# A visit's squares behind the next h copy on VectorE, h blocks strictly one after another, and a later first visit for batch 2

## The chip, the cores and the metric

The kernel runs on one core of a Trainium2 chip. The metric is the device time of one execution in microseconds (us); the time before is the median of eleven runs. Everything said of single instructions comes from one profiled execution.

## The reference

Eight batches of a squared-ReLU attention (12 heads, 448 positions, head size 64) feed one feed-forward layer with a squared ReLU between its two products:

```python
scores = scale * np.matmul(q, k.transpose(0, 1, 3, 2))
attn = np.maximum(scores, 0.0) ** 2 / S
x = np.matmul(attn, v)            # heads side by side: (8*448) x 768
h = x @ w_in                      # 768 -> 2048
r = np.maximum(h, 0.0)
out = (r * r) @ w_out             # 2048 -> 768
```

There is no softmax: a score is scaled, clipped at zero and squared, and so is each element of h.

## The kernel before

**Attention tiles.** A batch has three units of four heads, a unit has seven chunks of 64 keys, and a chunk of a unit is a *tile*: 21 tiles for a batch (`NB0`), 168 in all. For one tile TensorE makes the scores into a *slot* of PSUM (L234; there are two slots), ScalarE applies scale and ReLU into an fp16 tile `at` (L238), VectorE squares `at` in place (L306), and TensorE multiplies it with v (L252) into the two banks `avt`, which collect the seven tiles of a unit. After the seventh, the two banks are copied into `xt`, the feed-forward layer's input, as two of its six 128-row slices: on VectorE (L265), except that the first of the last unit's two copies goes to ScalarE for batches 0 and 1 (L262).

**A visit** (`visit`, L293) does such work for a list of tiles, mostly two: prefetches where a new unit begins, the scores and ReLUs of its tiles, perhaps the transposes of a later unit's q and k (`pe_transpose`), then up to three v products of *older* tiles (`av_some`; a tile is used two visits after its own), and last the squares of its own tiles. [...]

**Feed-forward.** An h block (`h_group(b, f)`, one of 16 for a batch) is six matmuls over the six slices of `xt` (L320) into one bank of the two-bank pool `mm`, then a ReLU copy from that bank into `g`. In batch 0 the copies of f = 0 and of odd f go to VectorE (L331); all others go to ScalarE (L335). After each odd f VectorE squares the two blocks' `g` (L338). When two batches are through, 14 o blocks of 16 matmuls each (L362), in the same two banks, give the pair's output, which ScalarE copies out (L384).

**The order** is written out by hand. The first batch's attention has a stage to itself, eleven visits (L403 to L419). From then on `steps` is the list of all h and o matmuls with a cost in model time for each, and `events` is a list of visits, transposes and prefetches with a due time; the loop at L482 issues an event before the first step that is an edge (the first matmul of an h block, any matmul of an o block) at or after its due time. `T_G` is the model time of an h block, `T_H` that of a batch's 16. Batch 1's attention is spread over batch 0's h blocks by `seq`; batches 2 and 3 get 21 visits spaced evenly (`gap`) from `at0` to a fixed end, and so on for the later pairs.

**Where batches begin.** The last unit of a batch gives slices 4 and 5 of `xt`, so the first four matmuls of an h block can run before it is there. Before the first visit of batch 1 the program issues four matmuls of f = 0, the v products that are left, four matmuls of f = 1, then the visit, then the last two matmuls of f = 0 and of f = 1. Batch 1's h blocks begin with the same interleaving of two (L469 and L470).

**Prefetch of units 6 and 7.** `prefetch(6)` casts q and k on GpSimd (L121), held until the h matmul issued last is done (`hold`), and transposes them by two DMAs in SyncE's queue (L135). `prefetch(7)` also loads unit 8's q and k and its own v. The tiles of unit 6 are the first of batch 2.

Of the kernel before, what the change touches and what calls it, by code (L numbers as in the profile page):

```python
# [17 lines left out]
def kernel(  # L18
# [9 lines left out]
    nc = tc.nc  # L28
# [19 lines left out]
    NF = FF // P  # L48
# [139 lines left out]
    def pe_transpose(n):  # L188
        srcs = q16s.pop(n)
        ts = new_qkt()  # L190
        ps = slot(FP16)

        def copy(i, eng):
            dst = ts[i].rearrange("p j c -> p (j c)")
            if eng == 0:
                nc.scalar.activation(out=dst, in_=pss[i][:, i, 0:J * P], func=AF.Copy)  # L196
            else:
                nc.vector.tensor_copy(dst, pss[i][:, i, 0:J * P])

        pss = [ps, slot(FP16) if n == 0 else ps]  # L200
        for i, src in enumerate(srcs):
            for j in range(J):
                for hh in range(2):
                    nc.tensor.transpose(  # L204
                        pss[i][64 * hh:64 * hh + 64, i, j * P:(j + 1) * P],
                        src[:, hh, j * D:(j + 1) * D], ident)
            if n == 0:
                copy(i, 1)
                warm(1)
        qkt[n] = ts  # L210
        if n == 3:
            return lambda: (copy(0, 0), copy(1, 0))
        if n > 0:
            copy(0, n < 3)
            copy(1, n < 3)
        return None
# [9 lines left out]
    def score(t, times=1):  # L226
        n, j = divmod(t, J)
        qT, kT = qkt[n]
        ps = slot(FP32)
        for hh in list(range(2)) * times:  # L230
            r = slice(64 * hh, 64 * hh + 64)
            for hp in range(2):
                c = slice(64 * hp, 64 * hp + 64)
                nc.tensor.matmul(  # L234
                    ps[c, hh, 0:S], lhsT=kT[r, j, c], rhs=qT[r, :, c],
                    start=True, stop=True)
        at = at_p.tile([P, 2, S], FP16, name="at", tag="at")
        nc.scalar.activation(out=at, in_=ps[:, :, 0:S], func=AF.Relu, scale=SK)  # L238
        ats[t] = at
        seen[t] = now[0]  # L240
# [28 lines left out]
    def av_some(lag=2, most=3):  # L269
        done = 0  # L270
        while av_order and done < most:
            t = av_order[0]
            if t not in seen or seen[t] > now[0] - lag:
                break
            av_order.popleft()
            av_round(t)
            done += 1
            if t % J == J - 1:
                break

    def prefetch(m):
        if m >= NUN:
            return
        if NPE + 2 <= m + 1 < NUN:
            load_qk(m + 1, nc.sync)
        cast_qk(m)
        if m > NPE:
            load_v(m)
        dma_transpose(m)

    copies: deque = deque()

    def visit(tiles, turn=None, lag=2, most=3):  # L293
        now[0] += 1
        for t in tiles:
            if t % J == 0 and t >= NPE * J:
                prefetch(t // J + 2)
        for t in tiles:
            score(t, 1 if "mm" in big else 2)
        later = pe_transpose(turn) if turn is not None else None  # L300
        ready = list(tiles)
        av_some(lag, most)
        if later:
            later()
        for t in ready:
            nc.vector.tensor_mul(ats[t], ats[t], ats[t])  # L306


    gts: dict = {}
# [1 line left out]
    def h_group(b, f):  # L311
        pr = b // 2
        z = (b % 2) * S
        cell = [None]

        def step(m):
            def run():
                if m == 0:
                    cell[0] = big["mm"].tile([P, 512], FP32, name="hps", tag="mm")
                held[:] = [nc.tensor.matmul(  # L320
                    cell[0][:, 0:S],
                    lhsT=w1[f // 4][:, m, (f % 4) * P:(f % 4 + 1) * P],
                    rhs=xts[b][:, m, :], start=(m == 0), stop=(m == NM - 1))]
                if m < NM - 1:
                    return
                gs = gts.setdefault(pr, [])
                if len(gs) <= f // 2:
                    gs.append(g_p.tile([P, 2, 2 * S], FP16, name="g", tag="g"))
                g = gs[f // 2][:, :, z:z + S]
                if b == 0 and (f % 2 == 1 or f == 0):  # L330
                    nc.vector.tensor_scalar(  # L331
                        out=g[:, f % 2], in0=cell[0][:, 0:S],
                        scalar1=0.0, scalar2=None, op0=ALU.max)
                else:
                    nc.scalar.activation(  # L335
                        out=g[:, f % 2], in_=cell[0][:, 0:S], func=AF.Relu)
                if f % 2 == 1:
                    nc.vector.tensor_mul(g, g, g)  # L338
            return run

        return [(0.1892, step(m), m == 0) for m in range(NM)]
# [10 lines left out]
    def o_steps(pr):  # L352
        steps = []
        cell = [None, None]

        def step(tb, hf, f):
            last = pr == B // 2 - 1 and tb == NT_PAIR - 1

            def run():
                if f == 0:  # L360
                    cell[0] = big["mm"].tile([P, 512], FP32, name="ops", tag="mm")
                nc.tensor.matmul(  # L362
                    cell[0][:, 0:HALF],
                    lhsT=gts[pr][f // 2][:, f % 2, tb * P:(tb + 1) * P],
                    rhs=w2[f // 4][:, f % 4, hf * HALF:(hf + 1) * HALF],
                    start=(f == 0), stop=(f == NF - 1))
                if f < NF - 1:
                    return
                if hf == 0:
                    cell[1] = osb_p.tile([P, DM], FP32, name="osb", tag="osb")  # L370
                z = hf * HALF
                if last and hf == 1:
                    h = HALF // 2
                    o2 = osb_p.tile([P, DM], FP32, name="osb", tag="osb")
                    nc.scalar.activation(  # L375
                        out=cell[1][:, z:z + h], in_=cell[0][:, 0:h],
                        func=AF.Copy, scale=CO)
                    nc.vector.tensor_scalar(  # L378
                        out=o2[:, z + h:DM], in0=cell[0][:, h:HALF],
                        scalar1=CO, scalar2=None, op0=ALU.mult)  # L380
                    store(pr, tb, cell[1], slice(z, z + h), nc.scalar)
                    store(pr, tb, o2, slice(z + h, DM), nc.sync)
                    return
                nc.scalar.activation(  # L384
                    out=cell[1][:, z:z + HALF], in_=cell[0][:, 0:HALF],
                    func=AF.Copy, scale=CO)
                if last:
                    store(pr, tb, cell[1], slice(0, HALF), nc.sync)
                elif hf == 1:
                    store(pr, tb, cell[1], slice(0, DM), nc.sync)  # L390
            return run

        for tb in range(NT_PAIR):
            for hf in range(2):
                for f in range(NF):
                    steps.append((0.1625, step(tb, hf, f), True))
        return steps
# [27 lines left out]
    big["mm"] = ctx.enter_context(tc.tile_pool(name="mmps", bufs=2, space=PSUM))  # L425


    f0, f1 = h_group(0, 0), h_group(0, 1)
    for _, fn, _ in f0[0:4]:
        fn()  # L430
    av_some(0, 9)
    for _, fn, _ in f1[0:4]:
        fn()
    visit([NB0, NB0 + 1])

    T_G = NM * 0.1892
    T_H = NF * T_G
# [4 lines left out]
    seq = [[2, 3], 4, [4, 5], [6, 7], [8, 9], 5, [10, 11], [12, 13], [14, 15],  # L442
           [16, 17], [18, 19], [20], []]
    for i, ts in enumerate(seq):
        at = (3 + i) * T_G
        if isinstance(ts, int):
            events.append((at, lambda n=ts: pe_transpose(n)))
        else:
            events.append((at, lambda ts=ts: visit([NB0 + t for t in ts])))
    events.append((T_H, lambda: av_some(0, 9)))  # L450

    for m in (6, 7):
        events.append((T_H + (1 + 3 * (m - 6)) * T_G, lambda m=m: prefetch(m)))
    at0 = T_H + 7 * T_G
    for pr in range(1, B // 2):
        t0 = 2 * NB0 * pr
        end = T_P * pr + T_H - 5.5
# [4 lines left out]
        at0 = end  # L462
    for i in range(3):
        events.append((at0 + 0.3 + i, lambda: visit([])))

    steps = [(0.1892, None, False)] * 8 + f0[4:] + f1[4:]
    for f in range(2, NF):
        steps += h_group(0, f)
    f0, f1 = h_group(1, 0), h_group(1, 1)  # L469
    steps += f0[0:4] + f1[0:4] + f0[4:] + f1[4:]  # L470
    for f in range(2, NF):
        steps += h_group(1, f)
    steps += o_steps(0)
    for pr in range(1, B // 2):
# [44 lines left out]
```

## Time and profile before

| | |
|---|---|
| median of eleven runs | 407.14 us (405.88 to 407.90) |
| profiled execution | 407.48 us, of which the span 405.6 us |
| TensorE busy, with waits inside matmuls | 393.5 us, 97% of the span |
| VectorE busy | 184.3 us, 45% |
| ScalarE busy | 237.8 us, 59% |
| GpSimd busy | 74.3 us, 18% |
| granted TensorE clock, mean | 0.996 |

The span runs from the first to the last recorded instruction; the time around it is 1.9 us here. "Waited" in the list of waits is idle time of an engine just before an instruction, put down to what came last. In the chain of waits each row is a start, a duration and the work on the path that ended last.

### The profile page before, as it was taken

How to read it: one execution, taken by the hardware profiler on the slowest of the kernel's cores; microseconds unless marked ns; L12 is line 12 of the kernel's file. 1: busy time of each engine (PE TensorE's matmuls, PEld its weight loads, DVE VectorE, ACT ScalarE, POOL GpSimd, SP SyncE). 2: the span in 40 equal slices, each digit the busy share in tenths (PEclk: the TensorE clock that was granted, in tenths of full speed). 3: DMA queues.
4: the chain of work that ended last, by engine and by line, in shares of the span. 5: the costliest groups of instructions: out<-in, count | busy, mean ns of one | idle time of the engine just before them, and what ended most of it. 6: DMA issues, size and time to landing. Idle time of an engine off the chain costs nothing.

```text
span 405.6 us, 7816 instructions
## 1 busy us (share of the span) xinstructions
PE 393.5 (97%) x3272; PEld 199.1 (49%) x3272; DVE 184.3 (45%) x295; ACT 237.8 (59%) x353; POOL 74.3 (18%) x94
## 2 busy tenths in 40 slices
PE   8897999999999999999999999999999999999995
PEld 3543444445555444445555544445555544556563
DVE  2975694563453476474244364564332445320000
ACT  3985884675565687775464577766554665441111
POOL 8544203340322062020022222020000000000000
PEclk9998999999999999999999999999999999999999
DMA  8999991996598696442589767253333110001333
GB/s 124 201 204 218 242 247 34 277 224 155 109 224 191 135 222 145 74 118 38 136 161 213 182 153 158 47 136 47 81 83 79 41 39 2 0 2 39 79 78 78
DMA packets 62497, 50.82 MB, mean 125 GB/s; under 512 B 35712, under 2 KB 58688, under 8 KB 62464
## 3 DMA queue, kind: packets, MB, share of 16 engines
q1 hardware_dynamic: 46752, 33.86, 34.9%
q0 software_dynamic: 15552, 16.39, 24.6%
q8 instruction: 25, 0.41, 0.4%
q10 hardware_dynamic: 160, 0.10, 0.1%
q14 instruction: 8, 0.07, 0.0%
HBM read 45.61 MB, written 11.01 MB: 140 GB/s over the span
## 4 chain that ended last, share of the span: by engine, by line
PE 89%; DVE 4%; ACT 4%; DMA 1%; issue 1%; POOL 1%; ACTq 0%
PE ops L362 37%; PE hps L320 34%; PE slot L234 9%; PE avt L252 7%; ACT at L238 3%; DVE at L306 2%; PE slot L204 1%; DMA kT<-ks 1%; PE slot L185 1%; DVE xt L265 1%; ACT qT L196 0%; DVE g L331 0%; ACT kT L196 0%; POOL ks L121 0%; DVE g L338 0%
## 5 line engine op out<-in xcount | busy, mean ns | idle before, releaser
L238 ACT ACTIVATE at<-slot 128x896 f16<-128x896 f32 x168 | 144.2, 918 | 50.6 <-PE slot L234 50.5
L320 PE MATMUL hps<-xt,w 128*128 128x448 f16 x768 | 155.5, 355 | 2.2 <-DVE g L331 2.0
L362 PE MATMUL ops<-w,g 128*128 128x384 f16 x896 | 152.3, 326 | 0.0
L306 DVE TENSOR_TENSOR at<-at 128x896 f16<-128x896 f16 x168 | 108.7, 666 | 90.9 <-ACT at L238 90.7
L362 PEld LDWEIGHTS <-g 128*128 128x128 f16 x896 | 84.8, 98 | 66.2 <-issue 12.5
L320 PEld LDWEIGHTS <-w 128*128 128x128 f16 x768 | 71.5, 98 | 81.0 <-issue 19.9
L335 ACT ACTIVATE g<-hps 128x448 f16<-128x448 f32 x119 | 64.8, 545 | 55.2 <-PE hps L320 54.9
L338 DVE TENSOR_TENSOR g<-g 128x896 f16<-128x896 f16 x64 | 43.7, 683 | 55.7 <-ACT g L335 55.2
L234 PE MATMUL slot<-qT,kT 64*64 64x448 f16 x756 | 54.4, 362 | 2.6 <-DMA kT<-ks 0.9
L384 ACT ACTIVATE osb<-ops 128x384 f32<-128x384 f32 x55 | 27.1, 492 | 50.5 <-PE ops L362 38.6
L121 POOL CAST qs<-qf 128x896 f16<-128x896 f32 x18 | 18.5, 1026 | 173.5 <-DMA qf<-in_q_dram 89.8
L252 PE MATMUL avt<-at,vt 64*64 64x448 f16 x672 | 47.7, 350 | 0.8 <-DVE xt L265 0.8
L265 DVE TENSOR_SCALAR xt<-avt 128x448 f16<-128x448 f32 x46 | 26.6, 618 | 26.5 <-PE avt L252 26.5
L234 PEld LDWEIGHTS <-kT 64*64 64x64 f16 x756 | 16.6, 105 | 32.9 <-issue 28.5
L252 PEld LDWEIGHTS <-vt 64*64 64x64 f16 x672 | 20.0, 107 | 14.3 <-issue 3.8
L121 POOL CAST ks<-kf 128x896 f16<-128x896 f32 x18 | 19.4, 1078 | 4.8 <-DMA kf<-in_k_dram 3.6
L97 POOL DMA_DIRECT2D vt<-in_v_dram x24 | 17.1, 713 | 2.7 <-DMA w<-in_moe_w_in_dram 1.2
L378 DVE TENSOR_SCALAR osb<-ops 128x192 f32<-128x192 f32 x1 | 0.4, 358 | 35.6 <-ACT osb L375 35.6
L331 DVE TENSOR_SCALAR g<-hps 128x448 f16<-128x448 f32 x9 | 5.5, 620 | 2.0 <-PE hps L320 2.0
L185 PE MATMUL slot<-zeros 128*128 128x448 f16 x12 | 4.8, 559 | 1.2 <-DVE zeros L161 1.2
L146 POOL DMA_DIRECT2D w<-in_moe_w_in_dram x8 | 5.4, 674 | 3.1 <-DMA w<-in_moe_w_in_dram 1.2
L91 POOL DMA_DIRECT2D q<-in_q_dram x6 | 4.5, 748 | 3.2 <-PE slot L234 1.8
(24 smaller groups left out, 38.5 us busy)
## 6 DMA issues: line engine op xcount, KB each, us to landing
out_dram<-osb SPq DMA_DIRECT2D x54, 192.0 KB, 2.7
qf<-in_q_dram SPq DMA_DIRECT2D x16, 448.0 KB, 5.1
kf<-in_k_dram SPq DMA_DIRECT2D x16, 448.0 KB, 5.8
vt<-in_v_dram POOLq DMA_DIRECT2D x24, 224.0 KB, 4.8
w<-in_moe_w_in_dram POOLq DMA_DIRECT2D x8, 384.0 KB, 11.9
w<-in_moe_w_out_dram POOLq DMA_DIRECT2D x4, 768.0 KB, 16.5
q<-in_q_dram POOLq DMA_DIRECT2D x6, 224.0 KB, 7.4
k<-in_k_dram POOLq DMA_DIRECT2D x6, 224.0 KB, 7.9
```

The source lines that it names most:

```text
L97: nc.gpsimd.dma_start(out=t, in_=heads(v, n))
L121: ins = nc.gpsimd.tensor_copy(t.rearrange("p j h d -> p h j d"), src.rearrange("p h (j d) -> p h j d", d=D))
L234: nc.tensor.matmul(ps[c, hh, 0:S], lhsT=kT[r, j, c], rhs=qT[r, :, c], start=True, stop=True)
L238: nc.scalar.activation(out=at, in_=ps[:, :, 0:S], func=AF.Relu, scale=SK)
L252: nc.tensor.matmul(ap[hp][64 * hh:64 * hh + 64, 0:S], lhsT=vt[r, hh, j * D:(j + 1) * D], rhs=at[r, hh, :], start=(j == 0), stop=(j == J - 1))
L265: nc.vector.tensor_scalar(out=dst, in0=ap[hp][:, 0:S], scalar1=CX, scalar2=None, op0=ALU.mult)
L306: nc.vector.tensor_mul(ats[t], ats[t], ats[t])
L320: held[:] = [nc.tensor.matmul(cell[0][:, 0:S], lhsT=w1[f // 4][:, m, (f % 4) * P:(f % 4 + 1) * P], rhs=xts[b][:, m, :], start=(m == 0), st ...
L335: nc.scalar.activation(out=g[:, f % 2], in_=cell[0][:, 0:S], func=AF.Relu)
L338: nc.vector.tensor_mul(g, g, g)
L362: nc.tensor.matmul(cell[0][:, 0:HALF], lhsT=gts[pr][f // 2][:, f % 2, tb * P:(tb + 1) * P], rhs=w2[f // 4][:, f % 4, hf * HALF:(hf + 1) * ...
L384: nc.scalar.activation(out=cell[1][:, z:z + HALF], in_=cell[0][:, 0:HALF], func=AF.Copy, scale=CO)
```

## The change

The squares of a visit are no longer issued at its end. They are put on a list, `due`, which `flush` issues: right after the copy of the next h block to end (before that pair's `g` square), or after the fourth matmul of an o block, or in the next visit ahead of its v products, whichever is issued first. While the first batch's attention has the core to itself (`"mm" not in big`) they are issued at once, as before. The two interleavings of f = 0 and f = 1 are gone: at the start of batch 0 four matmuls of f = 0 remain ahead of the v products and the visit, and its last two follow, and then f = 1 whole; batch 1 runs f = 0, f = 1 and so on in order. The due times in `seq` are set to 2.5 + i blocks, and the first visit of batch 2 becomes due at `T_H + 8 * T_G`, with the gaps up to the unchanged end a little smaller. No instruction is added or removed.

```diff
+    due: list = []
+
+    def flush():
+        for at in due:
+            nc.vector.tensor_mul(at, at, at)
+        due.clear()
+
     def visit(tiles, turn=None, lag=2, most=3):
         now[0] += 1
...
         later = pe_transpose(turn) if turn is not None else None
-        ready = list(tiles)
+        flush()
         av_some(lag, most)
         if later:
             later()
-        for t in ready:
-            nc.vector.tensor_mul(ats[t], ats[t], ats[t])
+        due.extend(ats[t] for t in tiles)
+        if "mm" not in big:
+            flush()
...
                     nc.scalar.activation(
                         out=g[:, f % 2], in_=cell[0][:, 0:S], func=AF.Relu)
+                flush()
                 if f % 2 == 1:
                     nc.vector.tensor_mul(g, g, g)
...
                     start=(f == 0), stop=(f == NF - 1))
+                if f == 3:
+                    flush()
                 if f < NF - 1:
                     return
...
-    f0, f1 = h_group(0, 0), h_group(0, 1)
+    f0 = h_group(0, 0)
     for _, fn, _ in f0[0:4]:
         fn()
     av_some(0, 9)
-    for _, fn, _ in f1[0:4]:
-        fn()
     visit([NB0, NB0 + 1])
...
-        at = (3 + i) * T_G
+        at = (2.5 + i) * T_G
...
-    at0 = T_H + 7 * T_G
+    at0 = T_H + 8 * T_G
...
-    steps = [(0.1892, None, False)] * 8 + f0[4:] + f1[4:]
-    for f in range(2, NF):
+    steps = [(0.1892, None, False)] * 4 + f0[4:]
+    for f in range(1, NF):
         steps += h_group(0, f)
-    f0, f1 = h_group(1, 0), h_group(1, 1)
-    steps += f0[0:4] + f1[0:4] + f0[4:] + f1[4:]
-    for f in range(2, NF):
+    for f in range(NF):
         steps += h_group(1, f)
```

## The prediction

> **What bounds the kernel now.** I read the engines' busy times first, then what TensorE waited for, then the chain of waits around each of those waits, then one-microsecond stretches with the granted clock.
>
> ```profile
> PE 393.5 (97%) x3272; PEld 199.1 (49%) x3272; DVE 184.3 (45%) x295; ACT 237.8 (59%) x353; POOL 74.3 (18%) x94
> PEclk9998999999999999999999999999999999999999
> PE hps L320 <- DVE g L331: 2.0, 1, 2.0
> ...
> PE slot L234 <- DMA kT<-ks: 0.9, 1, 0.9
> PE avt L252 <- DVE xt L265: 0.8, 4, 0.4
> ...
> PE hps L320 <- ACT g L335: 0.3, 1, 0.3
> ```
>
> TensorE is the bound and nearly gapless: a us taken from its idle time or its slow time is a us of the result, and work that other engines do beside it is free until it makes TensorE wait. The clock row has one weak digit, the fourth (30 to 41 us). The longest wait stands at its start:
>
> ```profile
> 30.82 0.92 ACT at L238
> 31.77 0.63 DVE at L306
> 32.39 0.54 DVE g L331
> 32.98 1.38 PE hps L320 x6
> 34.36 0.89 PE slot L234 x4
> 35.25 2.35 PE hps L320 x6
> ...
> 34.00:35.00 1.00, 1.00 (x10) 0.19 (x8) 0.12 (x1) 0.54 (x2) 0.50 (x2) 0.53 1.26 204
> 35.00:36.00 1.00, 1.00 (x7) 0.38 (x4) 0.12 (x1) 1.00 (x3) 0.82 (x2) 0.50 1.24 205
> ...
> 37.00:38.00 1.00, 1.00 (x18) 0.47 (x18) 0.68 (x2) 0.00 (x0) 0.42 (x1) 0.76 1.22 203
> ```
>
> The chain (start, us, what) says: ReLU of the second tile, its square, and only then the copy of h block 0, which frees the bank that block 2 waits for. The copy's data had been in PSUM since 31.0; it stood behind two squares in VectorE's queue. In the stretches the third number from the end is the granted clock: about half from 34.1 to 37.5, where the six matmuls of block 3 take 2.35 us. Six cost 1.17 at full clock (three blocks in 3.51 us, later in the chain).
>
> [...] the eleven times lie in two groups, five at 405.9 to 406.4 and six at 407.1 to 407.9, as such a penalty would make them. [...]
>
> **Part 1, the start of batch 0.** The common point is 28.71, the end of the v products before block 1's four matmuls. Before, the next transposes start at 37.53, 8.82 us later. In that time: 20 h matmuls at 0.195 = 3.9, two tile pairs of scores at 0.50 = 1.0, the 1.97 wait, and the rest, about 1.9, almost all half clock: block 3 costs 2.35 - 1.17 = 1.18 more and its scores 0.89 - 0.50 = 0.39 more, together 1.57. After, with the same durations: scores to 29.2; the last two matmuls of block 0 need slices 4 and 5, whose copies end at 29.36 (ScalarE) and 29.48 (VectorE), plus 0.1 for the signal: TensorE idles some 0.3 and ends block 0 at 29.8. Block 1 ends at 30.97. VectorE copies block 0 at 29.9 to 30.5, so block 2 runs at once to 32.1. The ReLUs start behind the ScalarE copy, at 29.36 instead of 30.01, and end at 31.1; the squares end at 31.8, block 1's copy at 32.4. Scores run to 32.6, block 3 finds its bank free by 0.2, and ends at 33.8. That is 5.1 us instead of 8.8: **-3.7** (2.1 of it the wait less the new idle, 1.6 the clock). Bounds: -3.2 if block 1's copy, behind squares that wait for ReLUs, is 0.5 later than I have it and so makes block 3 wait; -3.9 if the 0.3 idle hides. No gain at all would need the bank to be held by something else than that copy.
>
> **Part 2, odd blocks of batch 0.** On odd f, VectorE's order turns from square, square, copy, `g` square into copy, square, square, `g` square. The squares come later by the copy (0.54), and `g` with what follows by up to a square. Mostly that is covered: tiles are used two visits later. I walked the queue: at f = 7 the first product of a tile starts at 44.8 and its square would be done by 44.1; at f = 11 it is 53.9 against 52.9; at f = 15, 62.7 against 62.6, no cover left. The one place where VectorE already sets the end is f = 12 to 13:
>
> ```profile
> 55.77 0.62 DVE at L306
> 56.39 0.55 DVE g L331
> ...
> 56.96 0.62 DVE g L338
> 57.59 1.08 DVE xt L265 x2
> ```
>
> After: copy when block 11 is done (55.70), two squares and the `g` square, four times 0.54 in all, so `xt` starts at 57.87 instead of 57.51: **+0.4** on TensorE. Bounds 0.2 (VectorE is free earlier) to 0.8 (f = 15 waits too). Even f have their copies on ScalarE; there, and in every later batch, no VectorE instruction is issued between a visit's end and the next flush, so VectorE's order is what it was and the cost is nothing. The same holds for the flush at the fourth matmul of an o block: it adds no wait to TensorE.
>
> **Part 3, the start of batch 1.** Block 0 now needs slice 5 after five matmuls instead of nine.
>
> ```profile
> 64.54 0.54 ACT L262 ACTIVATE xt<-avt 128x448 f16<-128x448 f32 x1 [1.51 <-PE avt L252]
> 64.96 0.62 DVE L338 TENSOR_TENSOR g<-g 128x896 f16<-128x896 f16 x1
> 65.51 0.62 DVE L265 TENSOR_SCALAR xt<-avt 128x448 f16<-128x448 f32 x1
> 66.98 0.92 POOL L121 CAST qs<-qf 128x896 f16<-128x896 f32 x1 [23.45 <-PE hps L320]
> ```
>
> Blocks begin at 64.44. Slice 5 is there at 66.1 plus 0.1, so block 0 ends at 66.35, block 1 at 67.5, and block 2 starts there; before it started at 67.16, after a 0.25 wait for a copy that is now off the path: **+0.35**, bounds 0.2 and 0.7.
>
> **Part 4, unit 6 and the first visit of batch 2.** Before, the cast starts at 66.98 when both interleaved blocks are through, the transposed k lands at 73.83 (the transpose's row: 69.38 plus 4.45), and TensorE waits 0.88. After, the hold is on block 0's last matmul: cast at about 66.45, k at 73.3. The two casts and two transposes of `prefetch(6)` move one block forward on GpSimd and SyncE, which have nothing else queued there. The visit is due one block later, at 67.5 + 6 x 1.17 = 74.5. Margin 1.2 us: **-0.9**, bound -0.6. The visits of batches 2 and 3 move later by a block at first and by less each time (gap 2.77 instead of 2.82 us of model time), taking the loads of units 8 to 11, GpSimd's casts and SyncE's transposes with them; a unit's tiles come seven visits, over 20 us, behind its prefetch, and TensorE shows no wait in 330 us from there on: nothing. Loads ahead of batch 0's blocks have microseconds to spare: the last k that the transposes at 47 need was issued at 26.3, and the longest such load lands in 11.9; the last part of `w_in`, issued at 28.0 for block 12 at 56, lands within 19.3.
>
> **Sum:** -3.7 + 0.4 + 0.35 - 0.9 = -3.85 against the profiled execution's own 407.48 (405.6 span and 1.9 around it): 403.6. The median of the runs is 407.14, in the upper group with the profiled run, so the median after should be the same **403.6**; without the clock's penalty on both sides, 406.0 - 2.25 = 403.75 agrees.
>
> **Rivals.** (a) *The half clock stays*: it comes from the thin first 30 us and not from the gap, or the new idles trip it. [...] against: stretches from 9 to 26 us with TensorE only 0.4 to 0.8 busy show 1.00. Then 403.6 + 1.6 = 405.2. (b) *A new wait replaces the old*: block 3 waits for block 1's copy behind the squares, and f = 15 for a square: 3.2 + 0.6 - 0.8 - 0.7 = 2.3 gained, 405.2. For: margins of 0.2 and 0.1; against: they cost only their excess. (c) *Slower*: late squares starve the v products at the ten visits with tiles beside batch 0's h blocks. TensorE then waits in each. To cancel the gain, each must cost 3.85 / 10 = 0.39, and as f = 7 has 0.7 of cover, squares would have to be 1.1 us later than before instead of 0.54; at 1.3 it is 403.6 + 10 x 0.6 = 409.6. For: VectorE is already the bound at f = 12; against: from 24 to 76 us it sat idle 12 times before a square, 10.3 us in all, waiting for ScalarE, so the queue catches up. (d) *It doesn't do what it says*: the copy is bound by something behind the squares anyway, and parts 2 and 3 offset part 4: 407.3.
>
> **How the numbers follow.** The likeliest case, the sum, has 0.70; (a) 0.11, (b) 0.12, (c) 0.04, (d) 0.03. Bounds of the parts give 402.9 to 405.2 for the sum; (a) and (b) sit at the upper end, so the range is 402.8 to 405.3. A difference of 0.2%, 0.8 us, is about what a measurement can tell: faster 0.93, same 0.03, slower 0.04.
>
> **What would show it.** Right: no wait of h matmuls for `g` L331, no granted clock near 0.5 about 34 us, no wait of slot for kT, a wait of some 0.5 for `xt` inside block 0 of batch 1, and a longer `avt` wait for `xt` at f = 13. Wrong: a wait for `at` L306 ahead of v products in several visits (c), or a half clock without a gap (a).

## The result

Thirteen runs of the changed kernel have a median of 403.9 us (403.31 to 406.14) against 407.16 us of 48 runs of the kernel before: a ratio of 0.9928, interval 0.991 to 0.9945, so 0.7% less time (the ratio with its 95% interval is the recorded estimate; the two medians alone give 0.992). The forecast was 403.6, range 402.8 to 405.3.

The profiled execution took 404.5 us, of which the span is 402.6. First the engines' busy times and the granted clock by slice, from the page of the changed kernel:

```profile
PE 390.9 (97%) x3272; PEld 198.4 (49%) x3272; DVE 179.9 (45%) x295; ACT 237.6 (59%) x353; POOL 74.0 (18%) x94
PEclk9999999999999999999999999999999999999999
```

The instruction counts are unchanged. The weak digit of the clock row is gone; TensorE's busy time fell by 2.6 us although it does the same matmuls. Of that, 1.6 is the half clock, as an experiment below separates it. What it waited for (total, times, longest):

```profile
PE slot L204 <- DMA k<-in_k_dram: 1.3, 2, 1.1
...
PE avt L252 <- DVE xt L265: 1.1, 5, 0.4
...
PE hps L329 <- DVE xt L265: 0.6, 1, 0.6
PE slot L204 <- DMA q<-in_q_dram: 0.5, 1, 0.5
...
PE hps L329 <- ACT xt L262: 0.3, 1, 0.3
```

The waits of h matmuls for `g` (2.0) and of scores for kT (0.9) have gone. A wait for slice 5 of `xt` at the start of batch 1 (0.6) and one for slice 4 at the start of batch 0 (0.3) have come, and the one for `xt` ahead of v products grew from 0.8 to 1.1. The first and fourth lines are waits for loads in the first stage, which the change does not touch.

Cutting both profiled runs at the same TensorE instructions shows where the time went (us):

| stretch | before | after | difference |
|---|---|---|---|
| start to the twelve v products ahead of batch 1's first visit | 28.02 | 28.96 | +0.94 |
| to the transposes ahead of block 4 (part 1) | 9.51 | 5.88 | -3.63 |
| to the first h matmul of f = 13 (part 2) | 21.68 | 22.01 | +0.33 |
| to the first h matmul of batch 1 | 5.23 | 5.23 | 0 |
| to the first scores of batch 2, before plus one h block of 1.17 (parts 3 and 4) | 10.60 | 9.96 | -0.64 |
| to the end, before less that block | 330.56 | 330.56 | 0 |

The sum is -3.00, the difference of the two spans. The first row holds those load waits of 1.3 and 0.5, partly in place of other waiting. It is not of the change: in the ten profiles of the experiments below, whose first stage is the same, this stretch took 27.64 to 28.44. The rest is -3.94, where the prediction had -3.85.

The start of batch 0 in the chain of waits (start, us, what):

```profile
29.03 0.75 PE avt L252 x12
29.78 0.53 ACT xt L262
30.31 0.04 issue
30.36 2.81 PE hps L329 x14
33.16 0.50 PE slot L234 x8
33.67 1.24 PE hps L329 x6
34.91 0.92 PE slot L204 x28
```

The 14 matmuls are the last two of block 0 and blocks 1 and 2 without a gap. Ahead of them stands the one copy that they need, and block 3 takes 1.24 where it took 2.35.

### The profile page after: what moved, and what is told of

It reads as the page before. It is cut to its first block, busy times and chain, and to the rows that moved or that the text cites. A ratio compares the mean times of both kernels' runs of the same rounds, so it can differ in the third digit from the quotient of the medians.

```text
span 402.6 us, 7816 instructions
## 1 busy us (share of the span) xinstructions
PE 390.9 (97%) x3272; PEld 198.4 (49%) x3272; DVE 179.9 (45%) x295; ACT 237.6 (59%) x353; POOL 74.0 (18%) x94
## 4 chain that ended last, share of the span: by engine, by line
PE 90%; DVE 3%; ACT 2%; DMA 2%; POOL 1%; issue 1%; DVEq 0%; POOLq 0%; ACTq 0%
PE ops L372 37%; PE hps L329 36%; PE slot L234 9%; PE avt L252 7%; DMA k<-in_k_dram 2%; ACT at L238 1%; DVE at L298 1%; PE slot L204 1%; DVE xt L265 1%; ACT qT L196 0%; ACT kT L196 0%; DVE g L340 0%; POOL q L91 0%; DVE g L348 0%; POOL k L92 0%
## 5 line engine op out<-in xcount | busy, mean ns | idle before, releaser
L329 PE MATMUL hps<-xt,w 128*128 128x448 f16 x768 | 153.8, 353 | 0.9 <-DVE xt L265 0.6
L298 DVE TENSOR_TENSOR at<-at 128x896 f16<-128x896 f16 x168 | 107.3, 659 | 80.6 <-ACT at L238 80.5
L348 DVE TENSOR_TENSOR g<-g 128x896 f16<-128x896 f16 x64 | 41.1, 643 | 58.3 <-ACT g L344 58.0
L204 PE MATMUL slot<-ident,q 128*64 128x128 f16 x84 | 3.5, 222 | 1.6 <-ACT at L238 1.0
```

The costliest lines, as they stand in the source:

```text
L298: nc.vector.tensor_mul(at, at, at)
L329: held[:] = [nc.tensor.matmul(cell[0][:, 0:S], lhsT=w1[f // 4][:, m, (f % 4) * P:(f % 4 + 1) * P], rhs=xts[b][:, m, :], start=(m == 0), st ...
```

## Experiments

TensorE's mean granted clock is recorded for each run, and the runs fall in two groups by it: 0.996 and less, or 0.997 and more. That a part of the runs is slower by this clock is the mechanism in question here, so both groups are given; the upper one is called "at the full clock". Ahead of TensorE's last matmul the half clock itself is seen in two profiles alone, those of the kernel before and of the gap filled; of runs without a profile only the mean is known. The mean also counts the end of the span, where no matmul is left: in the gap-filled profile the clock is at half from 404.94 us on, two us after the last matmul. So the size of a mean below 0.997 does not price a drop.

Of 104 runs of the kernel before, made beside the experiments, 55 are at the full clock, median 405.97, and 49 below it, median 407.46. The median over both moves with their shares, from 406.43 to 407.16 between the sets of runs of this one kernel. The 18 runs of the changed kernel at the full clock (two sets) have a median of 403.64, so at the full clock the change gains 2.33; the rest of the gain in the medians over all runs goes with the half clock, which the change makes rare (1 of 19 runs below the full clock, against 49 of 104).

### Parts alone

**Squares alone** (on the kernel before: `due` and `flush`, nothing else):

```diff
...
-        for t in ready:
-            nc.vector.tensor_mul(ats[t], ats[t], ats[t])
+        due.extend(ats[t] for t in tiles)
...
```

> The kernel before with the later squares alone: the interleavings and the first visit of batch 2 stay as they were. Theory (the bank waits for a copy that is queued behind squares, and the gap brings the half clock): block 0's copy runs as soon as its matmuls end, block 2 starts at about 31.3 instead of 33.0 in the frame of the profiled run before, at most 0.3 us of waiting is left, the half clock does not come, and batch 0's f = 13 loses 0.35; the wait for kT of 0.9 stays. Net -3.3 + 0.35 = about -2.9 against a run with the half clock: 404.2. Rival (the order of the blocks is what counts): the wait of h matmuls for g stays near 2 us and the time near 407.

Measured: 404.9 (ratio 0.9944, 0.9921 to 0.9967); 1 of 10 runs below the full clock, the others at 404.89. The waits:

```profile
PE slot L234 <- DMA kT<-ks: 0.7, 1, 0.7
...
PE hps L328 <- DVE g L339: 0.3, 1, 0.3
```

The wait for the copy is down to 0.3 as expected. The profiled run took 404.19, as expected, but the median is 0.7 above; why the runs lie above their profiled one is not shown. From the v products to the transposes it took 6.30 us, so this part gains 3.21 of the 3.63, clock included. Moving the squares is most of part 1. Of the whole gain at the full clock it is less than half: 405.97 to 404.89, which is 1.08 of the 2.33.

**Blocks one by one alone** (the changed kernel, with the squares flushed at the visit's end and the first visit of batch 2 at the seventh block):

```diff
         due.extend(ats[t] for t in tiles)
-        if "mm" not in big:
-            flush()
+        flush()
...
-    at0 = T_H + 8 * T_G
+    at0 = T_H + 7 * T_G
```

> The changed kernel with the squares issued at the visit's end again and the first visit of batch 2 due as before, so the blocks one after another alone. Theory: block 0's copy is still behind two squares, which end at about 31.9, so block 2 waits some 1.5 us (start 32.5) instead of 2.0, and the half clock still comes in a part of the runs. Batch 1 start +0.4, kT wait gone through the earlier prefetch -0.9. Net about -0.6 + 0.4 - 0.9 = -1.1: 406.0 median, with two groups of times. Rival (block order is what counts): about 404, no wait for g.

Measured: 405.1 (0.9968, 0.9954 to 0.9982), 0.9 better than I expected; 2 of 22 runs below the full clock, the others at 405.09.

```profile
PE hps L328 <- DVE g L339: 1.1, 1, 1.1
...
PE hps L328 <- DVE xt L265: 0.6, 1, 0.6
PE slot L234 <- DMA kT<-ks: 0.6, 1, 0.6
```

Two expectations fell. The gap is 1.1, not 1.5, and with so short a gap (and the 0.25 ahead of block 0's end) few runs are below the full clock. And the wait for kT is not gone: it is 0.6 with the earlier prefetch, where the profiled run before had 0.9 and the squares alone, which prefetch no earlier, 0.7.

**The later visit alone** (on the kernel before):

```diff
-    at0 = T_H + 7 * T_G
+    at0 = T_H + 8 * T_G
```

> The kernel before with the first visit of batch 2 one h block later alone. Theory: the wait of the scores for kT of 0.9 us disappears and nothing else changes: 406.3, two groups of times 1.5 apart. Rival (a wait that only moves): a wait of the same size shows elsewhere and the time stays at 407.1.

Measured: 406.24 (0.9975, 0.9957 to 0.9993). At the full clock 10 runs, median 405.05, which is 0.92 below the 405.97 of the kernel before; below it 12 runs, 406.74. No wait for kT is in the profile, and none came in its place. This profiled run had the gap of 2.0 and yet the full clock after it (stretches of one microsecond: busy time of TensorE, its weight loads, VectorE, ScalarE and GpSimd, then the granted clock, DMA share and GB/s):

```profile
31.00:32.00 1.00, 0.07 (x1) 0.00 (x0) 0.80 (x2) 0.79 (x1) 0.33 (x1) 1.00 1.23 202
32.00:33.00 1.00, 0.00 (x0) 0.00 (x0) 1.00 (x3) 0.00 (x0) 0.39 (x1) 1.00 1.27 203
33.00:34.00 1.00, 0.97 (x6) 0.48 (x5) 0.96 (x2) 0.00 (x0) 0.32 (x1) 1.00 1.26 203
34.00:35.00 1.00, 1.00 (x12) 0.29 (x11) 0.17 (x1) 0.57 (x2) 0.89 (x2) 1.00 1.25 202
```

It gives the price of the gap without the clock. From the v products to the transposes this run took 7.92 us, the profiled run before 9.51, the changed kernel 5.88. So the 3.63 of part 1 are 2.04 of standing still and 1.59 of half clock.

### Is it the gap that brings the half clock?

**The gap filled** (on the kernel before):

```diff
+    def fill():
+        ps = av_ps[0].tile([P, 512], FP32, name="fil", tag="av")
+        for _ in range(9):
+            nc.tensor.matmul(ps[:, 0:S], lhsT=zeros[:, 0:P], rhs=zeros,
+                             start=True, stop=True)
...
-    steps = [(0.1892, None, False)] * 8 + f0[4:] + f1[4:]
+    steps = [(0.1892, None, False)] * 8 + f0[4:] + f1[4:] + [(0.0, fill, False)]
```

> The kernel before with nine matmuls on zeros, into a bank that nothing reads, put into the wait ahead of block 2 of batch 0 (nothing of the reference's computation is changed). The wait for the copy is as long as before, but TensorE is active in it. Theory (the half clock comes from that gap): no granted clock of 0.5 about 34 us, all runs in the lower group, 405.9, that is 1.2 to 1.6 below the upper group; median 1.2 lower. Rival (the half clock comes from the thin stretch before): clock and both groups stay, median 407.

Measured: 408.66 (1.003, 1.0008 to 1.0051; the ratio is without one run of 411.72), slower, and 13 of 22 runs below the full clock. By the numbers both theories failed. The waits and the stretches show why:

```profile
PE slot L234 <- DMA kT<-ks: 2.0, 1, 2.0
...
73.00:74.00 1.00, 0.21 (x4) 0.18 (x8) 0.00 (x0) 0.00 (x0) 0.00 (x0) 0.92 1.12 246
74.00:75.00 1.00, 1.00 (x9) 0.13 (x2) 0.00 (x0) 0.59 (x1) 0.00 (x0) 0.50 1.17 233
75.00:76.00 1.00, 1.00 (x4) 0.46 (x3) 0.62 (x1) 1.00 (x2) 0.00 (x0) 0.50 0.97 324
76.00:77.00 1.00, 1.00 (x4) 0.42 (x3) 0.62 (x1) 0.13 (x1) 0.31 (x1) 0.50 1.57 318
77.00:78.00 1.00, 1.00 (x6) 0.43 (x5) 0.30 (x1) 0.54 (x1) 0.70 (x2) 0.87 0.88 177
```

The clock is at 1.00 about 34 us, as the theory has it. But in this run the wait for kT had grown to 2.0, and the half clock came after that gap. The place of the trouble had moved, so this run did not separate the theories. The wait grew by 1.08 us. SyncE spent 2.20 us on issuing the transpose of q ahead of that of k, where the profiled run before had 1.31, and k then landed 4.6 us after its issue instead of 4.4: together that is about the 1.08. Why SyncE took longer is open.

**The gap filled and the later visit** (the same filling, `at0 = T_H + 8 * T_G`) takes the second place away too; its twin is the later visit alone.

> The nine matmuls on zeros in the wait ahead of block 2 of batch 0, and the first visit of batch 2 one block later, on the kernel before: both places where TensorE can stand still for 2 us are then gone or filled (nothing of the reference's computation is changed). Its twin is e3, which has the later visit without the filling and two groups of times, about 405.0 and 406.7. Theory (the half clock comes from these gaps): one group at 405.1, no clock of 0.5 in the profile. Rival (it comes from the thin first stage, or matmuls on zeros don't count as activity): two groups as in e3, median above 406.

Measured: 405.12 (0.9977, 0.9958 to 0.9995); 2 of 22 runs below the full clock, where the twin had 12 of 22. At the full clock the medians are the same, 405.07 and 405.05. The nine matmuls stand in the gap, and the wait for the copy that is left is 0.27:

```profile
30.84 1.87 PE L469 MATMUL fil<-zeros 128*128 128x448 f16 x9
32.97 1.29 PE L320 MATMUL hps<-xt,w 128*128 128x448 f16 x6 [0.27 <-DVE g L331]
```

So the gap is what puts half of the runs below the full clock, 12 of 22 with it open and 2 of 22 with it filled; the thin first stage, which is the same in both, is not, and nine matmuls on zeros were enough to keep those runs up. One part of the expectation missed: it is not one group. 7 of the 20 runs at the full clock lie from 406.1 to 408.3, where the twin's ten end at 405.8. They have no profile, so that scatter stays open, and the filling may not be free of other effects.

**Why half of the runs.** The profiles show this of stretches in which TensorE had no work, and of the granted clock there:

| run | TensorE idle (us) | granted clock |
|---|---|---|
| kernel before, wait for the copy | 1.97, up to 32.98 | 0.50 from 34.06 to 37.47 |
| gap filled, wait for kT | 1.96, up to 73.79 | 0.50 from 73.84 to 77.26 |
| gap filled, end of the work | 2.02, from the last matmul to the drop | 0.50 from 404.94 |
| later visit alone, wait for the copy | 1.97, up to 33.03 | 1.00 |
| blocks alone, wait for the copy | 1.14, up to 32.37 | 1.00 |
| kernel before, end of the work | 4.18, up to the end of the span | 1.00 |
| changed kernel, end of the work | 4.18, up to the end of the span | 1.00 |

The same gap of 1.97 was followed by the half clock in one profile and not in another, and 4.18 us without a matmul at the end of two spans brought none up to there. So the length of a gap alone does not decide it; what does, and so why it is about half of the runs, is not shown. What is shown are the shares in these runs: below the full clock are 49 of 104 of the kernel before (47%), 12 of 22 with the gap of 1.97 alone (55%), and 2 of 22 with a gap of 1.1.

The gap is not the only thing that can lower the mean. In the changed kernel and the eight experiments without an unfilled gap of 2 us, 9 of 101 runs are below the full clock too. None of the nine was profiled, so what lowered it there is open.

### The costs inside the change

**Old order from block 3 on** (the changed kernel, flush ahead of the copy for f of 3 and more in batch 0):

```diff
+                if b == 0 and f > 2:
+                    flush()
                 if b == 0 and (f % 2 == 1 or f == 0):
                     nc.vector.tensor_scalar(
```

> The changed kernel with the flush ahead of the copy again for f of 3 and more in batch 0, so the squares keep their place before the copies except at f = 0. Theory (part 2 costs 0.33 us, at f = 13): the wait for xt at f = 13 falls back to 0.4 in all, time 0.3 under the changed kernel's, about 403.4. Rival (the later squares also help elsewhere in batch 0): no gain, or 0.3 and more slower.

Measured: 403.33 (0.9916, 0.989 to 0.9942), with the wait of v products for `xt` at 0.8 again instead of 1.1, and 21.67 us in the stretch of part 2, against 22.01 in the changed kernel and 21.68 before. **Batch 1 interleaved** (the changed kernel with that one interleaving kept):

```diff
-    for f in range(NF):
+    f0, f1 = h_group(1, 0), h_group(1, 1)
+    steps += f0[0:4] + f1[0:4] + f0[4:] + f1[4:]
+    for f in range(2, NF):
         steps += h_group(1, f)
```

> The changed kernel with the interleaving of f = 0 and f = 1 kept at the start of batch 1. Theory (part 3 costs 0.4 us): the wait of h matmuls for xt of 0.6 is gone and a wait of 0.25 for g on ScalarE is back, 0.4 us less; the k of unit 6 then comes 0.3 later and the visit 0.4 earlier, which leaves about 0 of cover, so up to 0.4 of it can go into a wait for kT: 403.2 to 403.8. Rival (nothing is lost at the start of batch 1): as the changed kernel, 403.9.

Measured: 403.39 (0.9923, 0.9898 to 0.9948). From batch 1's first matmul to the first scores of batch 2 it took 9.62 us instead of 9.96; no wait for kT came. Each of the two is within the other's interval and the changed kernel's, so it is the stretches of the profiles that show the 0.3, not the medians. **Both, and the visit at the ninth block:**

> Both of these undone together (squares before the copies for f of 3 and more, interleaving at the start of batch 1), and the first visit of batch 2 at the ninth block, so that kT has a block more of cover. Theory: 0.33 + 0.4 less than the changed kernel, about 403.1. Rival: the later visits of batches 2 and 3 come closer together and give something back, 403.9.

Measured: 403.03 (0.9922, 0.9898 to 0.9946); 8 of 10 runs at the full clock, median 402.95, against 403.64 of 18 such runs of the changed kernel in two sets. So 0.7 less at the full clock, as the two costs add to; but two runs below the full clock blur it, and over all runs this version is not shown to beat the changed kernel.

**The visit back at the seventh block** (the changed kernel), and its twin, the changed kernel again on the same chip:

```diff
-    at0 = T_H + 8 * T_G
+    at0 = T_H + 7 * T_G
```

> The changed kernel with the first visit of batch 2 due at the seventh block again. Theory (the later visit, not the earlier prefetch, takes the wait for kT away, since e2 with the earlier prefetch alone still waited 0.6): a wait of 0.4 to 0.6 for kT is back and the time is that much above the changed kernel on the same chip. Rival (part 4 as predicted, the earlier prefetch alone is enough for half of it): a wait of 0.3 or less, time within 0.3 of the changed kernel's.

> The changed kernel itself on the chip of e5, as its twin, and for the share of runs in which the clock drops. Theory: 403.7 to 403.9, clock under 0.997 in at most 1 run of 10, where the kernel before has it in 4 to 5 of 10. Rival (the low share so far was luck): 3 and more of 10, median above 404.5.

Measured: 404.25 (0.9937, 0.9914 to 0.996) for the one, 403.6 (0.9917, 0.9898 to 0.9936) for the other. At the full clock the medians are 404.12 and 403.6, 0.5 apart, though the profile shows a wait for kT of only 0.2:

```profile
70.42 0.57 PE L234 MATMUL slot<-qT,kT 64*64 64x448 f16 x8 [0.20 <-DMA kT<-ks]
```

The wait sided with the rival, the time seemingly with the theory. But the two profiled runs are 0.5 apart as well (spans of 402.1 and 401.6), and 0.29 of that arises ahead of batch 1's first visit, which the edit does not touch: 28.20 us against 27.91, with a wait of 0.3 for a load of k. What is left is about the size of the wait, so the medians do not settle it for the theory. The twin's six runs are all at the full clock, its profile has no wait for loads of q and k, and its span is 401.6, a microsecond below the 402.6 of the first profile. Together with the first thirteen, 1 of 19 runs of the changed kernel fell below the full clock, where 49 of 104 did before.

## Why the prediction was right

**Part 1** carried it: predicted -3.7, measured -3.63, and the split was right as well, 2.1 and 1.6 predicted, 2.04 and 1.59 measured. The timeline of VectorE after has the copy of block 0 first, then two squares, then the copy of block 1, as walked through:

```profile
30.93 0.62 DVE L340 TENSOR_SCALAR g<-hps 128x448 f16<-128x448 f32 x1 [0.50 <-PE hps L329]
31.47 1.15 DVE L298 TENSOR_TENSOR at<-at 128x896 f16<-128x896 f16 x2
32.54 0.62 DVE L340 TENSOR_SCALAR g<-hps 128x448 f16<-128x448 f32 x1
```

The step that decided was to follow the copy back to what stood ahead of it in its own queue, and to price the slow matmuls behind the gap as part of the gap. Rival (a), that the half clock stays, fell with the filled gap and the later visit, and with 1 of 19 runs of the changed kernel; (d), that something else holds the copy, fell with the lines above. The check against the lower group of the times, 403.75, agrees with the 403.64 of the runs at the full clock.

**Part 2**, predicted +0.4, measured +0.33, at the place named:

```profile
53.01 0.62 DVE g L340
53.63 1.07 DVE at L298 x2
54.70 0.54 DVE g L348
55.23 1.07 DVE xt L265 x2
56.31 0.04 issue
56.35 0.57 PE avt L252 x6
```

Copy, two squares, `g` square, `xt`: the squares now stand between the copy and what TensorE waits for. No wait for a square appears in any visit, at f = 15 either, so rival (c) had nothing to stand on, and (b) took nothing from the gain: block 3 waits for no bank.

**Parts 3 and 4** together, predicted -0.55, measured -0.64. Part 3, by the timeline of the start of batch 1:

```profile
62.08 1.12 PE L329 MATMUL hps<-xt,w 128*128 128x448 f16 x5
...
63.15 0.62 DVE L265 TENSOR_SCALAR xt<-avt 128x448 f16<-128x448 f32 x1
63.82 8.29 PE L329 MATMUL hps<-xt,w 128*128 128x448 f16 x43 [0.62 <-DVE xt L265]
64.24 0.92 POOL L121 CAST qs<-qf 128x896 f16<-128x896 f32 x1 [18.95 <-PE hps L329]
```

Five matmuls, a wait of 0.62 for slice 5 (TensorE starts 0.05 behind the end of its copy, where I had allowed 0.1 for the signal), then 43 without a gap up to the visit at block 8. Undoing it took 0.34 off. In part 4 the size was right and one step was loose: I let the k of unit 6 land a fixed time behind its cast, 6.85 us, and gave the block 8 visit 1.2 us of margin. In the changed kernel the transpose of k is issued at 66.67 and lands 4.4 later, 6.8 behind the cast and about 1.0 ahead of the visit at 72.04; its twin has 0.9. But in the blocks-alone run k landed 7.3 behind its cast, which would leave about 0.5, and in the gap-filled run 7.9, which would leave none. So the margin held with some luck. Which half of part 4 did it is shown in part: with the earlier prefetch alone the wait is 0.2 (the visit back) or 0.6 (the blocks alone) instead of 0.9, and in every profile with the later visit it is gone.

**The later batches**, costed at nothing, cost nothing: 330.56 us on both sides.

**The sum.** -3.85 against -3.94, each group of parts within 0.1 us of its forecast: the agreement is one of parts, not of errors that cancel. One sum of bounds was off: the parts' own lower bounds give 403.1, not 402.9, which the range covers. The median of the runs before was luck on the side of the gain. The two groups are near half each, so it could have stood at 406.4 as well, and the same 403.6 after would have been a gain of 2.8 instead of 3.5. The forecast of the time after does not rest on it.

## What to carry to other kernels

VectorE took its work as it was issued: in the kernel before, the copy of block 0 had its data by 31.0 and stood behind two squares until 32.39, even while VectorE sat idle for 0.18 us ahead of the second; issued ahead of two squares, after the change, it started at 30.93 and the first of them at 31.47. So issue first what another engine's buffer is waiting for, and what has cover behind it; a square that is needed two visits later has no business ahead of a copy that frees a bank for the next matmul. Price a gap on TensorE by the matmuls behind it too: here a gap of 2 us cost 1.5 us more (medians of 407.46 and 405.97) in about half of the runs (49 of 104). And when one gap is closed, look for the next that can do the same, or an experiment on the first will read as a failure.

## What the runs showed of the hardware

- A TensorE gap of 1.97 us was followed by half the clock for 3.4 us, from 34.06 to 37.47, in the profile of the kernel before, and by none in that of the later visit alone. One of 1.96 was followed by it for 3.4 us, from 73.84 to 77.26, in that of the gap filled. What decides is not shown. By the mean clock, 49 of 104 runs of the kernel before are below the full clock; its only other wait above 0.3 past the first stage is the one for kT. With that gap alone it is 12 of 22, and 2 of 22 when the gap was filled, and 2 of 22 when it was 1.1 long.
- With nine matmuls on zeros in that gap, 20 of 22 runs were at the full clock, though these matmuls compute nothing; with the gap open it was 10 of 22.
- The transposed k of unit 6 landed 4.2 to 4.9 us after its issue in the profiles of the first four experiments. What moved more was the time that SyncE spent on issuing the transpose of q ahead of it: 1.3 us in three of them and 2.20 in the one that waited longest.
